# A seven-product MLP behind an attention: copies of two transposed tiles, and the order of the last products, moved

## The chip, the cores and the metric

The kernel runs on one core of one Trainium2 chip. The metric is the device time of one execution in microseconds (us), as the median of three runs. The core has five engines that run side by side and wait for one another by semaphores: TensorE (PE; its weight loads are PEld), VectorE (DVE), ScalarE (ACT), GpSimd (POOL) and SyncE (SP), the last of which only issues DMAs here. Each engine works off its own queue in order: an instruction that waits holds up everything queued behind it on that engine.

## The reference

An attention whose scores are masked by a hash of q and k, followed by a block that mixes with a Fourier transform, normalises, and applies a two-layer MLP. What matters here is the second part, with x of shape (4 batches, 768 rows, 512 columns):

```python
X = np.fft.fft(np.fft.fft(x, axis=1), axis=2)
u = x + np.real(X)
un = (u - mean(u)) / np.sqrt(var(u) + 1e-06)
ch = np.maximum(un @ w_ch1, 0.0) @ w_ch2      # 512 -> 2048 -> 512
return u + ch
```

## The kernel before, in words

**Stages.** First comes the attention for all four batches (to about 338 us). Then each batch b = 0 to 3 goes through `mlp7` (line 1442), which applies the two layers of the MLP; `front` (line 1055), the Fourier part of the next batch, runs beside it. Products of large blocks are done by a scheme that needs seven products of quarter blocks where the plain one needs eight. The quarters of the left and right factor are added and subtracted first, and the seven results are added and subtracted into the four quarters of the result.

**First layer.** Its result is the tile `hall`, with the quarters c11, c12, c21 and c22. It is made in two halves of the 2048 hidden features. Batches 0 and 1 use seven products per block row (lines 1538 to 1563). Batches 2 and 3 go through `two_levels` (line 1646), where each of the seven products (A11, S2, A12, S1, S3, A22, S4) is again split into seven leaves, j = 0 to 6. `ring_ahead` (line 1575) fixes the order of the 49 leaves of a half: product n and leaf j are sorted by 7n + 2j, so that the end of one product overlaps the beginning of the next. A leaf is four matmul instructions in the profile (line 1739). Its left factor comes by DMA into a ring of 12 slots. A product has three PSUM tiles, each a bank: `run`, used by leaves 0, 2, 4 and 6, one for leaf 1, and one for leaves 3 and 5. Leaf 2 adds into `run` in place, so it may start only when leaf 0's result has been read out; the same holds for leaves 4 and 6.

`placed` (line 1685) takes a leaf's result out of PSUM. The first six products of the order go into a quarter or a spare tile (table `to`, line 1666), in part by copies on ACT (line 1669), in part by adds on DVE (line 1675). The last product, S4, is added straight into its final place c12 by seven adds on DVE, with a ReLU on ACT (line 1672) behind four of them. `behind` (line 1712) holds the adds of whole quarters that follow the seventh leaf of a product.

**Second layer.** `outer7` (line 1365) is called for each half and works on three pairs of row tiles, j = 0 to 2: tile j, whose sum row is u, and tile j + 3, whose sum row is v. A pair is seven products of eight matmuls (line 1392). `tile_sums` (line 1366) makes the left sums on DVE: s1 from c12 and c22 (line 1376), s2 from s1 and c11 (line 1377), s3 from c11 and c12 (line 1378). The names a11, a12, a21, a22 stand there for parts of c11, c21, c12 and c22. So c21 goes only into the product `a12` and into the sum of line 1416. Results are added into u and v, scaled by the row's 1/deviation (line 1404), and in the second half stored to the output (`store`, line 939; on POOL's queue for batches 0 to 2, on SP's for batch 3).

**The tiles u and v.** `across` (line 1187) transposes a row tile of x on PE into a PSUM tile, and ACT copies it out (line 1193) into a buffer `ut[T]`. These buffers are shared between batches: the copy for batch b must wait until the store of batch b - 1 has read the same buffer. In batches 2 and 3, tiles 0, 3, 1 and 4 are copied in `first_parts`; tiles 2 and 5 at the beginning of `two_levels` (lines 1650 and 1651), ahead of the first leaf. `last_parts` (line 1171) then makes the last sums of the right factor on DVE.

**What sets the order.** The attention's order is as written. For all that comes after it, a planner puts each engine's instructions in order when the program is built; it prefers what stands earlier in the program, and takes something later when the earlier one is not ready by its own estimate. Where the code says `with in_turn():` (line 694) the instructions inside are queued behind the last recorded copy or ReLU of ACT and the last recorded add of DVE. PSUM has eight banks, and after the attention all tiles in it come from one pool of eight (line 1217).

Of the kernel before, what the change touches and what calls it, by code (L numbers as in the profile page):

```python
# [17 lines left out]
ALU = mybir.AluOpType  # L18
AX = mybir.AxisListType

P = 128
# [11 lines left out]
GT = GTT * P  # L33
# [450 lines left out]
def _main(  # L484
# [13 lines left out]
    nc = tc.nc  # L498
# [191 lines left out]
    ET = mybir.EngineType  # L690
# [493 lines left out]
        parted(b, xv[:, 0:1, 1], 6)  # L1184
        third(xv[:, :, 1])

    def across(b, T, u):

        x = xs[b]
        ps = pt([P, NDC, P], f"un{b}_{T}")  # L1190
        for c in range(NDC):
            nc.tensor.transpose(ps[:, c, :], x[:, c, T * P : (T + 1) * P], ident)
        nc.scalar.copy(u, ps.rearrange("p c n -> p (c n)"))

    def spread(b, T, u):

        bs = wt([P, 6], F32, "bs", f"bs{b}_{T}")
        nc.vector.bn_stats(bs, u)  # L1198
        mv = wt([P, 2], F32, "mv", f"mv{b}_{T}")
        nc.vector.bn_aggr(mv, bs)  # L1200
        rs = wt([P, 1], F32, "rs", f"rs{b}_{T}", NT)
        nc.gpsimd.tensor_scalar(rs, mv[:, 1:2], 1e-6, None, op0=ALU.add)
        nc.gpsimd.tensor_tensor(rs, rs, mhalf, op=ALU.pow)
        return rs
# [124 lines left out]
    def blocks2():  # L1329

        for half in range(2):
# [18 lines left out]
            for i in range(7):  # L1350
# [11 lines left out]
                )  # L1362
                yield

    def outer7(b, half, hall, ut, rs, s1s):
        def tile_sums(j):
            if half == 0:
                for T in (j, j + GT):
                    if T not in rs:
                        rs[T] = spread(b, T, ut[T])  # L1370
            a11, a12, a21, a22 = (
                hall[:, i, :, (j + g * GT) * P : (j + g * GT + 1) * P]
                for g in range(2) for i in range(2)
            )
            s1, s2 = s1s[j % 2], s2s[j % 2]
            nc.vector.tensor_tensor(s1, a21, a22, op=ALU.add)  # L1376
            nc.vector.tensor_tensor(s2, s1, a11, op=ALU.subtract)
            nc.vector.tensor_tensor(a21, a11, a21, op=ALU.subtract)
            return a11, a12, a21, a22, s1, s2

        nxt = tile_sums(0)
        for j in range(GT):
            a11, a12, s3, a22, s1, s2 = nxt
            u, v = ut[j], ut[j + GT]
            ru, rv = rs[j], rs[j + GT]

            def product(a, i, ps=None):
                start = ps is None
                if start:
                    ps = pt([P, HD], f"o{b}_{half}_{j}_{i}")  # L1390
                for r in range(HF // 2):
                    nc.tensor.matmul(  # L1392
                        ps, a[:, r], right7[i][:, r], start=start and r == 0,
                        stop=r == HF // 2 - 1, skip_group_check=not start,
                    )
                if j == GT - 1 and (b < B - 1 if half else b > 0):
                    nc.sync.dma_start(right7[i], bd[1 - half, i])
                return ps

            low, high = slice(0, HD), slice(HD, DM)  # L1400
            t6, t7 = (temps[j % 2][:, i] for i in range(2))

            def add(t, r, cols, src):
                done_by[ET.DVE] = nc.vector.scalar_tensor_tensor(  # L1404
                    t[:, cols], src, r, t[:, cols], op0=ALU.mult, op1=ALU.add
                )


            px = product(a11, B11)
            add(u, ru, low, px)  # L1410
            yield
            p2 = product(a12, B21)
            add(u, ru, low, p2)
            if half:
                store(b, j, u, low)
            nc.vector.tensor_tensor(a12, a12, s2, op=ALU.subtract)
            product(s2, T2, px)
            done_by[ET.Activation] = nc.scalar.copy(t6, px)  # L1418
            yield
            add(u, ru, high, t6)  # L1420
            p5 = product(s1, T1)
            add(v, rv, high, p5)
            product(s3, T3, px)
            done_by[ET.Activation] = nc.scalar.copy(t7, px)  # L1424
            add(v, rv, high, t7)
            if half:
                store(b, j + GT, v, high)
            yield
            if j < GT - 1:
                nxt = tile_sums(j + 1)  # L1430
            product(a12, B22, p5)
            add(u, ru, high, p5)
            if half:
                store(b, j, u, high)
            yield
            product(a22, T4, px)
            add(v, rv, low, px)
            yield
            if half:
                store(b, j + GT, v, low)  # L1440
# [133 lines left out]

    def ring_ahead():

        order = [A11, S2, A12, S1, S3, A22, S4]
        leaves = sorted(
            (half, 7 * n + 2 * j, i, j)
            for half in range(2)  # L1580
            for n, i in enumerate(order)
            for j in range(7)
        )
        fetched = [0]

        def fetch():
            if fetched[0] < len(leaves):
                half, _, i, j = leaves[fetched[0]]
                j = LEAVES[j]
                if isinstance(j, str):  # L1590
                    a, k = int(j[1]) - 1, int(j[2]) - 1
                    f = half * HF // 2 + a
                    src = ad[f : f + 3 : 2, i, :, k].rearrange("g p m -> p g m")
                else:
                    src = ad2[half, i, j]
                nc.sync.dma_start(ring[fetched[0] % NR], src)
                fetched[0] += 1

        for _ in range(NR):
            fetch()  # L1600
        return leaves, fetch
# [44 lines left out]
    def two_levels(b, right, ut, ss):  # L1646

        leaves, fetch = rings.pop(b)
        ut += [u4[b], wt([P, DM], F32, "u", f"u{b}_5", 2)]
        for T in (2, 5):  # L1650
            across(b, T, ut[T])
        last_parts(b)
        parts = {}
        for i, r in right.items():
# [8 lines left out]
        (c11, c12), (c21, c22) = (  # L1663
            [hall[:, i, :, g * HALF : (g + 1) * HALF] for g in range(2)] for i in range(2)
        )
        to = {A11: c12, S2: q0, A12: q1, S1: c22, S3: q0, A22: q1, S4: c12}

        def copy(d, s_):
            done_by[ET.Activation] = nc.scalar.copy(d, s_)  # L1669
# [4 lines left out]
        def add(d, x, y):  # L1674
            done_by[ET.DVE] = nc.vector.tensor_tensor(d, x, y, op=ALU.add)  # L1675
# [9 lines left out]
        def placed(i, j, ps):  # L1685

            y = to[i]
            y00, y01, y10, y11 = (
                y[:, a::2, c * HH : (c + 1) * HH] for a in range(2) for c in range(2)
            )  # L1690
            run, p2, p5 = (ps.get(n) for n in range(3))
            if i == S4:
                d = (y00, y00, y01, y11, y11, y01, y10)[j]
                add(d, d, (run, p2, run, p5, run, p5, run)[j])
                if j in (1, 4, 5, 6):
                    relu(d)
            elif j == 0:
                copy(y00, run)
            elif j == 1:
                add(y00, y00, p2)  # L1700
            elif j == 2:
                copy(y01, run)
            elif j == 3:
                copy(y11, p5)
            elif j == 4:
                add(y11, y11, run)
            elif j == 5:
                add(y01, y01, p5)
            else:
                copy(y10, run)  # L1710

        def behind(i):

            if i == S2:
                added(c21, c12, q0)
            elif i == A12:
                added(c11, c12, q1, relu)
            elif i == S1:
                added(c12, c21, c22)
            elif i == S3:  # L1720
                added(c21, c21, q0)
                added(c22, c22, c21, relu)
            elif i == A22:
                added(c21, c21, q1, relu)

        rs = {}

        def inner(half):
            banks_ = {}
            for n, (h_, _, i, j) in enumerate(leaves):  # L1730
                if h_ != half:
                    continue
                ps = banks_.setdefault(i, {})
                at_bank = (0, 1, 0, 2, 0, 2, 0)[j]
                start = at_bank not in ps
                if start:
                    ps[at_bank] = pt([P, 2, HH], f"h{b}_{half}_{i}_{at_bank}")
                for g in range(2):
                    nc.tensor.matmul(  # L1739
                        ps[at_bank][:, g], ring[n % NR][:, g], parts[i][j],  # L1740
                        start=start and g == 0, stop=g == 1, skip_group_check=True,
                    )
                fetch()
                placed(i, j, ps)
                if j == 6:
                    behind(i)
                if n in (24, 32):
                    T = 0 if n == 24 else GT
                    with in_turn():
                        rs[T] = spread(b, T, ut[T])  # L1750
                if n % 49 % 4 == 3:
                    yield
# [120 lines left out]
```

## Time and profile before

| | |
|---|---|
| median of 3 runs (lowest, highest) | 1011.06 us (1009.11, 1013.58) |
| the profiled execution's own time | 1011.05 us |
| its span in the profile | 1009.3 us |
| attention until about | 338 us |
| first layer of batch 2: first half, second half begin at | 693.74 us, 769.81 us |
| first layer of batch 3: first half, second half begin at | 860.70 us, 933.49 us |
| share of the span: PE, DVE, ACT, POOL | 98%, 72%, 48%, 10% |
| mean granted TensorE clock | 0.997 |

How to read it: times are us from the span's start; lines such as L1739 are lines of the kernel before. In a timeline a row is a run of like instructions: start, time until the last one's modelled end, engine, line, operation, output<-inputs, shape, count, and in brackets how long the engine stood idle before it and what released it. Matmuls overlap in the pipeline, so their pace is read from one row's start to the next row's start, not from the second column. A wait list names who waited for whom, the total in us, how often, and the longest.

### The profile page before, as it was taken

How to read it: one execution, taken by the hardware profiler on the slowest of the kernel's cores; microseconds unless marked ns; L12 is line 12 of the kernel's file. 1: busy time of each engine (PE TensorE's matmuls, PEld its weight loads, DVE VectorE, ACT ScalarE, POOL GpSimd, SP SyncE). 2: the span in 40 equal slices, each digit the busy share in tenths (PEclk: the TensorE clock that was granted, in tenths of full speed). 3: DMA queues.
4: the chain of work that ended last, by engine and by line, in shares of the span. 5: the costliest groups of instructions: out<-in, count | busy, mean ns of one | idle time of the engine just before them, and what ended most of it. 6: DMA issues, size and time to landing. Idle time of an engine off the chain costs nothing.

```text
span 1009.3 us, 15350 instructions
## 1 busy us (share of the span) xinstructions
PE 986.1 (98%) x5505; PEld 692.2 (69%) x5505; DVE 724.4 (72%) x1272; ACT 483.1 (48%) x933; POOL 96.7 (10%) x193
## 2 busy tenths in 40 slices
PE   8999999999999999999999999998999999899997
PEld 5444444444444756866885785897989899888986
DVE  4788898878986597778653686455897846693672
ACT  5787877878766465055035323212633521330420
POOL 3000000000000011320212130011220002010000
PEclk9999999999999999999999999999999999999999
DMA  9545362554510448567645495106838603743701
GB/s 145 122 96 110 87 160 53 123 96 100 127 45 10 151 120 286 168 191 265 204 154 170 139 328 172 54 21 214 261 98 277 185 22 109 219 117 105 228 28 46
DMA packets 207141, 141.37 MB, mean 140 GB/s; under 512 B 128464, under 2 KB 190416, under 8 KB 207056
## 3 DMA queue, kind: packets, MB, share of 16 engines
q1 hardware_dynamic: 196464, 106.48, 38.4%
q0 software_dynamic: 9024, 33.43, 10.8%
q8 instruction: 46, 0.75, 0.3%
q10 hardware_dynamic: 1568, 0.39, 0.2%
q14 instruction: 39, 0.32, 0.1%
HBM read 111.94 MB, written 28.31 MB: 139 GB/s over the span
## 4 chain that ended last, share of the span: by engine, by line
PE 87%; DVE 4%; DMA 3%; issue 3%; ACT 1%; POOL 1%; SPq 0%; DVEq 0%; POOLq 0%; ACTq 0%
PE o L1392 25%; PE oo L875 13%; PE h L1739 13%; PE sc L858 12%; PE h_px L1500 6%; PE h_p L1500 5%; PE sc L848 4%; PE cs L1073 3%; PE A L1102 2%; PE B L1102 2%; DMA zraw<-in_moe_w_ch_dram 2%; PE sum L895 1%; PE bits L812 1%; DMA out_dram<-w 1%; DVE bs L1198 1%
## 5 line engine op out<-in xcount | busy, mean ns | idle before, releaser
L1392 PE MATMUL o<-w,h 128*128 128x256 f32 x960 | 217.5, 379 | 0.1
L1392 PEld LDWEIGHTS o<-w,h 128*128 128x128 f32 x960 | 180.7, 190 | 24.6 <-DVE u L1404 0.7
L865 ACT ACTIVATE pk<-sc 128x768 f32<-128x768 f32 x192 | 152.6, 813 | 34.8 <-PE sc L858 31.4
L858 PE MATMUL sc<-qt,kt 64*128 64x384 f32 x768 | 155.5, 482 | 0.0
L875 PE MATMUL oo<-pk,vn 128*64 128x385 f32 (+1 forms) x768 | 134.4, 492 | 0.0
L932 DVE TENSOR_TENSOR acc<-acc,pk 128x1536 f32<-128x1536 f32 x63 | 110.1, 1748 | 3.1
L875 PEld LDWEIGHTS oo<-pk,vn 128*64 128x64 f32 x768 | 50.9, 136 | 81.1 <-issue 79.2
L858 PEld LDWEIGHTS sc<-qt,kt 64*128 64x128 f32 x768 | 69.5, 188 | 30.5 <-issue 30.0
L1418 ACT COPY tq<-o 128x256 f32<-128x256 f32 x24 | 8.9, 373 | 149.8 <-PE o L1392 149.8
L1404 DVE SCALAR_TENSOR_TENSOR w<-o,rs,w 128x256 f32<-128x256 f32 x88 | 42.2, 480 | 49.3 <-PE o L1392 48.6
L1739 PE MATMUL h<-sums,w 128*128 128x192 f32 x336 | 61.0, 328 | 6.5 <-ACT h L1669 6.5
L1739 PEld LDWEIGHTS h<-sums,w 128*128 128x128 f32 x336 | 55.5, 190 | 8.0 <-ACT h L1669 7.5
L848 PEld LDWEIGHTS <-kk 33*128 33x128 bf16 x384 | 19.6, 93 | 50.8 <-issue 28.6
L1739 PE MATMUL h<-x,w 128*128 128x192 f32 x256 | 52.4, 330 | 0.9 <-DVE h L1675 0.9
L1392 PE MATMUL o<-w 128*128 128x256 f32 x176 | 42.7, 381 | 4.1 <-DVE w L1376 4.1
L1392 PE MATMUL o<-w,tq 128*128 128x256 f32 x192 | 45.5, 380 | 0.4 <-DVE w L1404 0.4
L1739 PEld LDWEIGHTS h<-x,w 128*128 128x128 f32 x256 | 43.4, 192 | 2.7 <-DVE h L1675 2.0
L1424 ACT COPY tq<-o 128x256 f32<-128x256 f32 x24 | 8.9, 373 | 72.8 <-PE o L1392 69.7
L1675 DVE TENSOR_TENSOR h<-h,h 128x384 f32<-128x384 f32 x52 | 28.6, 551 | 20.1 <-PE h L1739 13.3
L1392 PEld LDWEIGHTS o<-w,tq 128*128 128x128 f32 x192 | 36.3, 190 | 5.9 <-DVE w L1404 0.8
L1739 PE MATMUL h<-w 128*128 128x192 f32 x192 | 40.2, 333 | 0.0
L1392 PEld LDWEIGHTS o<-w 128*128 128x128 f32 x176 | 32.9, 190 | 9.7 <-issue 3.3
(210 smaller groups left out, 1635.6 us busy)
## 6 DMA issues: line engine op xcount, KB each, us to landing
w<-ad SPq DMA_DIRECT2D x252, 128.0 KB, 2.6
w<-bd SPq DMA_DIRECT2D x42, 512.0 KB, 4.9
zraw<-in_moe_w_ch_dram SPq DMA_DIRECT2D x16, 512.0 KB, 4.5
zraw<-in_moe_w_ch_dram POOLq DMA_DIRECT2D x16, 512.0 KB, 4.0
bd<-w SPq DMA_DIRECT2D x14, 512.0 KB, 5.7
vn<-in_v_dram SPq DMA_DIRECT2D x32, 192.0 KB, 3.1
qn<-in_q_dram SPq DMA_DIRECT2D x116, 48.0 KB, 3.2
kn<-in_k_dram SPq DMA_DIRECT2D x58, 96.0 KB, 3.0
```

Of the source, the lines that this page charges most:

```text
L848: nc.tensor.matmul(pss[g][:, h, 0:HALF], kk[r, ks], bits[1][r] if g else bits[0][r, h], start=start, stop=not start,)
L858: nc.tensor.matmul(pss[g][:, h, 0:HALF], kt[rows, ks], qt[rows, g * HALF : (g + 1) * HALF], start=early, stop=not early,)
L865: nc.scalar.activation(pk[:, g, :, 0:HALF], pss[g][:, :, 0:HALF], AF.Exp, scale=SCALE)
L875: nc.tensor.matmul(oos[g][h * D : (h + 1) * D, 0:w], nat["v", n][:, (2 * c + h) * D : (2 * c + h + 1) * D], pk[:, g, h, 0:w], start=(c == ...
L932: nc.vector.tensor_tensor(acc, (first[:, :, :, 0:HALF] if c == 1 else acc), new, op=ALU.add)
L1073: nc.tensor.matmul(ps[:, pc + 2 * lo : pc + 2 * hi - 1 : 2], z[:, cp, pc, par, t * P : (t + 1) * P], ch[:, cp, pc, lo:hi], start=(cp == 0) ...
L1102: nc.tensor.matmul(ps[:, cols], F[:, par, k, t, j * P : (j + 1) * P], sq[:, t, k, cols], start=(t == 0), stop=(t == 1),)
L1392: nc.tensor.matmul(ps, a[:, r], right7[i][:, r], start=start and r == 0, stop=r == HF // 2 - 1, skip_group_check=not start,)
L1404: done_by[ET.DVE] = nc.vector.scalar_tensor_tensor(t[:, cols], src, r, t[:, cols], op0=ALU.mult, op1=ALU.add)
L1500: nc.tensor.matmul(ps, left[:, k], right[i][:, k], start=start and k == 0, stop=k == 1, skip_group_check=not start,)
L1675: done_by[ET.DVE] = nc.vector.tensor_tensor(d, x, y, op=ALU.add)
L1739: nc.tensor.matmul(ps[at_bank][:, g], ring[n % NR][:, g], parts[i][j], start=start and g == 0, stop=g == 1, skip_group_check=True,)
```

## The change

Three things are changed. In `two_levels` the transposes of tiles 2 and 5 stay where they are, but their copies from PSUM are handed back as functions and called inside the first half of the first layer, behind the leaves at places 10 and 14 of the order, under `in_turn`. The order of the seven products becomes A11, S2, A12, S1, S3, S4, A22: A22 is now the last and is added straight into c21, while S4 goes through the spare tile `q1` into c12. In `outer7` the order of the seven products of a pair becomes a11, s1, s2, a12, s3, (a12 - s2), a22, where it was a11, a12, s2, s1, s3, (a12 - s2), a22; the difference a12 - s2 is written over s2 instead of over a12; and `tile_sums` becomes a function of its own, called for the first pair of batches 2 and 3 already in the first layer, behind leaf 5 of A22. The count of instructions on each engine stays as it is.

```diff
-    def across(b, T, u):
+    def across(b, T, u, later=False):
         x = xs[b]
         ps = pt([P, NDC, P], f"un{b}_{T}")
         for c in range(NDC):
             nc.tensor.transpose(ps[:, c, :], x[:, c, T * P : (T + 1) * P], ident)
-        nc.scalar.copy(u, ps.rearrange("p c n -> p (c n)"))
+        def end():
+            nc.scalar.copy(u, ps.rearrange("p c n -> p (c n)"))
+        if later:
+            return end
+        end()
...
+    def tile_sums(b, half, hall, ut, rs, s1s, j):
+        if half == 0:
+            for T in (j, j + GT):
+                if T not in rs:
+                    rs[T] = spread(b, T, ut[T])
+        a11, a12, a21, a22 = (
+            hall[:, i, :, (j + g * GT) * P : (j + g * GT + 1) * P]
+            for g in range(2) for i in range(2)
+        )
+        s1, s2 = s1s[j % 2], s2s[j % 2]
+        nc.vector.tensor_tensor(s1, a21, a22, op=ALU.add)
+        nc.vector.tensor_tensor(s2, s1, a11, op=ALU.subtract)
+        nc.vector.tensor_tensor(a21, a11, a21, op=ALU.subtract)
+        return a11, a12, a21, a22, s1, s2
+
+    early = {}
+
     def outer7(b, half, hall, ut, rs, s1s):
...
-        nxt = tile_sums(0)
+        nxt = early.pop((b, half), None) or tile_sums(b, half, hall, ut, rs, s1s, 0)
...
             px = product(a11, B11)
             add(u, ru, low, px)
             yield
+            p5 = product(s1, T1)
+            add(v, rv, high, p5)
+            product(s2, T2, px)
+            done_by[ET.Activation] = nc.scalar.copy(t6, px)
+            add(u, ru, high, t6)
+            nc.vector.tensor_tensor(s2, a12, s2, op=ALU.subtract)
+            yield
             p2 = product(a12, B21)
             add(u, ru, low, p2)
             if half:
                 store(b, j, u, low)
-            nc.vector.tensor_tensor(a12, a12, s2, op=ALU.subtract)
-            product(s2, T2, px)
-            done_by[ET.Activation] = nc.scalar.copy(t6, px)
-            yield
-            add(u, ru, high, t6)
-            p5 = product(s1, T1)
-            add(v, rv, high, p5)
             product(s3, T3, px)
...
-                nxt = tile_sums(j + 1)
-            product(a12, B22, p5)
+                nxt = tile_sums(b, half, hall, ut, rs, s1s, j + 1)
+            product(s2, B22, p5)
...
-        order = [A11, S2, A12, S1, S3, A22, S4]
+        order = [A11, S2, A12, S1, S3, S4, A22]
...
-        for T in (2, 5):
-            across(b, T, ut[T])
+        ends = [across(b, T, ut[T], True) for T in (2, 5)]
...
-        to = {A11: c12, S2: q0, A12: q1, S1: c22, S3: q0, A22: q1, S4: c12}
+        to = {A11: c12, S2: q0, A12: q1, S1: c22, S3: q0, S4: q1, A22: c21}
...
-            if i == S4:
+            if i == A22:
...
-            elif i == A22:
-                added(c21, c21, q1, relu)
+            elif i == S4:
+                added(c12, c12, q1, relu)
...
+                if n in (10, 14):
+                    with in_turn():
+                        ends.pop(0)()
+                if i == A22 and j == 5:
+                    early[b, half] = tile_sums(b, half, hall, ut, rs, ss, 0)
```

More of the change, by code (lines that the diff above doesn't have):

```diff
@@ L1363, in blocks2 @@
                 yield
-    def outer7(b, half, hall, ut, rs, s1s):
[L1366 to L1379, printed above, removed]
-        nxt = tile_sums(0)
+    def tile_sums(b, half, hall, ut, rs, s1s, j):
[13 more added lines that the diff above has]
+    early = {}
+    def outer7(b, half, hall, ut, rs, s1s):
+        nxt = early.pop((b, half), None) or tile_sums(b, half, hall, ut, rs, s1s, 0)
         for j in range(GT):
```

## The prediction

> **What bounds the kernel now.** I read the page's first part, then the list of PE's waits, then the timeline around each of them.
>
> ```profile
> span 1009.3 us, 15350 instructions
> PE 986.1 (98%) x5505; PEld 692.2 (69%) x5505; DVE 724.4 (72%) x1272; ACT 483.1 (48%) x933; POOL 96.7 (10%) x193
> PE h L1739 <- ACT h L1669: 6.5, 2, 3.8
> PE o L1392 <- DVE w L1376: 4.1, 4, 1.3
> PE h L1739 <- DVE h L1675: 0.9, 2, 0.5
> 564.99 36.26 PE o L1392 x168
> ```
>
> PE sets the time. The last row, from the chain of work, is one half of the second layer of batch 1: 168 matmuls in 36.26 us, 0.216 us each with no gap. No instruction of PE is removed, so all that can be won is PE's idle and slow time, and the three wait rows name nearly all of it in the code that the diff touches: 6.5 us at the first layer behind a copy of ACT, 4.1 us at the second layer behind s1 (L1376), 0.9 us at leaves behind DVE. Now the first of them, in batch 2:
>
> ```profile
> 692.12 0.54 POOL L947 DMA_DIRECT2D out_dram<-w  x1 [0.71 <-DVE w L1404]
> 693.84 0.54 POOL L947 DMA_DIRECT2D out_dram<-u  x1 [1.18 <-DVE u L1404]
> 697.99 0.59 ACT L1193 COPY w<-un 128x512 f32<-128x512 f32 x1 [7.95 <-DMA out_dram<-w]
> 698.47 0.48 ACT L1669 COPY h<-h 128x384 f32<-128x384 f32 x1
> 698.99 0.59 ACT L1193 COPY u<-un 128x512 f32<-128x512 f32 x1
> 693.74 1.47 PE L1739 MATMUL h<-x,w 128*128 128x192 f32 x8
> 699.01 1.74 PE L1739 MATMUL h<-sums,w 128*128 128x192 f32 x8 [3.81 <-ACT h L1669]
> 704.04 0.81 PE L1739 MATMUL h<-x,w 128*128 128x192 f32 x4
> 699.65:703.05 3.40, 3.40 (x14) 3.40 (x13) 0.00 (x0) 1.44 (x3) 0.00 (x0) 0.59 0.28 77
> ```
>
> The copy of tile 2 waits 7.95 us for batch 1's store out of the same buffer, issued at 692.12. Behind it in ACT's queue stands the copy of leaf 0, which leaf 2 needs, so PE does leaves 0 and 1 (8 matmuls) and stands for 3.81 us. The last row (PE, PEld, DVE, ACT, POOL busy; granted clock, DMA share, GB/s) adds the second half of the damage: after the idle time the granted clock is 0.59. Batch 3 has the same stall, shorter, and the second half of each batch starts without these copies (the first row here is the ring's loads, median us to landing last):
>
> ```profile
> w<-ad SPq DMA_DIRECT2D x252, 128.0 KB, 2.6
> 860.70 1.47 PE L1739 MATMUL h<-x,w 128*128 128x192 f32 x8
> 864.88 1.57 PE L1739 MATMUL h<-sums,w 128*128 128x192 f32 x8 [2.71 <-ACT h L1669]
> 868.23 0.81 PE L1739 MATMUL h<-x,w 128*128 128x192 f32 x4
> 863.86 0.59 ACT L1193 COPY w<-un 128x512 f32<-128x512 f32 x1 [7.18 <-DMA out_dram<-w]
> 933.49 1.46 PE L1739 MATMUL h<-x,w 128*128 128x192 f32 x8
> 938.23 0.81 PE L1739 MATMUL h<-x,w 128*128 128x192 f32 x4
> ```
>
> **Part 1: the two copies move behind leaves 10 and 14.** Between the first and the last PE row of each start lie the same 28 matmuls. They take 938.23 - 933.49 = 4.74 us in an undisturbed half, 704.04 - 693.74 = 10.30 us in batch 2 and 868.23 - 860.70 = 7.53 us in batch 3. The stalls cost 5.56 and 2.79 us, together **8.35 us**. Do the copies wait again where they go? A leaf is four of the 28 matmuls, 0.68 us, so leaf 10 ends 11 x 0.68 = 7.4 us after the start. That is 701.1 in batch 2, with the store landed by 697.99: 3 us of margin; and 868.1 against 863.86, 4 us, in batch 3. The other store (tile 5's, issued 693.84) was in by 698.99 and its copy comes four leaves later, at 703.9. Ring loads (128 KB each) will now start while the stores are under way; I let that eat 1 to 2 us of the margin. What is then late next is only leaf 2 behind leaf 0's copy, as in the second halves, which is in the 4.74 us. The copies hold two of eight PSUM banks for 11 to 15 leaves. By then A11 and S2 have opened six more at most, and A11's second bank is free after one add, so I cost it at nothing; bound: a bank freed one add of DVE (0.55 us) late at each start, 1.1 us. In ACT's stream they are 2 x 0.59 us beside gaps; the copy queued behind each is needed four leaves (2.6 us) later: nothing.
>
> How much of this a timed execution holds is less sure for the clock: the stall's 5.56 us are 3.81 idle and 1.75 slow. By the Trainium skill, "TensorE: Matmul & The Clock Gate", Part 1, the clock halves after an idle window of about 3.4 us, and the windows run freely; so by it a stall of 3.81 us would close the gate in some executions only. The trace has it closed after 3.81 us and open after 2.71 us, and agrees so far; what the rule would give is rival 5.
>
> **Part 2: A22 last, s1 early.** Today's end of the first layer, batch 3, second half (behind one row of the page on the adds into u and v):
>
> ```profile
> L1404 DVE SCALAR_TENSOR_TENSOR w<-o,rs,w 128x256 f32<-128x256 f32 x88 | 42.2, 480 | 49.3 <-PE o L1392 48.6
> 963.62 0.59 PE L1392 MATMUL o<-w,h 128*128 128x256 f32 x2
> 964.70 1.89 PE L1392 MATMUL o<-w,h 128*128 128x256 f32 x8
> 967.10 0.59 PE L1392 MATMUL o<-w,h 128*128 128x256 f32 x2
> 967.54 0.81 PE L1739 MATMUL h<-sums,w 128*128 128x192 f32 x4
> 968.19 1.03 PE L1392 MATMUL o<-w,h 128*128 128x256 f32 x4
> 970.48 1.53 PE L1392 MATMUL o<-w 128*128 128x256 f32 x6 [1.27 <-DVE w L1376]
> 966.61 0.54 DVE L1675 TENSOR_TENSOR h<-h,h 128x384 f32<-128x384 f32 x1
> 968.39 0.56 DVE L1675 TENSOR_TENSOR h<-h,h 128x384 f32<-128x384 f32 x1 [0.53 <-PE h L1739]
> 968.98 0.52 ACT L1672 ACTIVATE h<-h 128x384 f32<-128x384 f32 x1 [0.56 <-DVE h L1675]
> 969.65 1.28 DVE L1376 TENSOR_TENSOR w<-h 128x512 f32<-128x512 f32 x2
> 895.10 1.03 PE L1392 MATMUL o<-w,h 128*128 128x256 f32 x4
> 896.55 0.92 PE L1739 MATMUL h<-x,w 128*128 128x192 f32 x4 [0.42 <-DVE h L1675]
> 898.38 1.46 PE L1392 MATMUL o<-w,h 128*128 128x256 f32 x6
> 900.61 1.53 PE L1392 MATMUL o<-w 128*128 128x256 f32 x6 [0.77 <-DVE w L1376]
> ```
>
> s1 hangs on the last leaf: leaf (967.54 to 968.19), add 968.39, ReLU 968.98, s1 969.65, PE 970.48. By starts, four matmuls from 968.19 end at 969.05: 1.43 us lost. In the first half (last four rows) 0.93 us is lost at 900.61 and 0.59 at 896.55. Batch 2 has the same waits (the wait list counts four and two). So about 2 x 1.43 + 2 x 1.52 = 5.9 us stand here.
>
> With A22 last, s1 needs c12 and c22, done one product earlier: it can follow the fifth leaf's add, at about 968 instead of 969.65. But the cover shrinks too. Today PE fills the gaps between the last leaves with both products a11 and a12: 12 matmuls before the last leaf, 4 behind. a12 needs c21, which is now the late quarter, so only the 8 of a11 are left: 4 x 0.216 = 0.86 us of new idle before the last leaf, whose own time is set by DVE's add at 966.61 as today. Behind it, s1's product starts at once or up to 0.3 us late. I get about 0.9 to 1.1 us lost in place of 1.43 to 1.52, and less if DVE takes that add ahead of the first result of the second layer (L1404, 0.48 us). I take a gain of **0.55 us** at each of the four places, **2.2 us**. Bounds: all 5.9 us go; or s1 comes no earlier, and a product less of cover (1.73 us) makes each place worse by that: -6.9 us.
>
> **Part 3: the new order in all pairs.** Between pairs nothing shows: the planner makes a later pair's sums far ahead (the two L1376 at 969.65 are for two pairs), each reuse of a PSUM bank keeps a whole product between read and write, and a12 - s2 has two products of cover, 3.5 us, for an operation of s1's shape (0.69 us below). What is left are the four half starts of batches 0 and 1, where s1 is wanted after one product, not two. Worst is batch 0's second half:
>
> ```profile
> 471.25 3.62 PE L1392 MATMUL o<-w,h 128*128 128x256 f32 x16
> 471.84 0.93 ACT L1523 ACTIVATE h<-h 128x384 f32<-128x384 f32 x2
> 472.93 0.69 DVE L1376 TENSOR_TENSOR w<-h 128x512 f32<-128x512 f32 x1
> ```
>
> s1 is done at 473.62; a11 ends at 471.25 + 1.73 = 472.98: 0.6 to 0.8 us of idle, unless the planner puts a12 in between. The other three have s1 in time. I take **-0.4 us** (bounds 0 and -0.8 with a little for the first half of batch 0). Stores are the same in number; one of four comes two products later, under PE's work.
>
> **Sum:** 8.35 + 2.2 - 0.4 = 10.15 us, from the profiled execution's 1011.05 (span 1009.3 and 1.75 around it; the median is 1011.06): **1001 us**.
>
> **The rivals.**
> 1. All waits vanish, the ends of the first layer too: 8.35 + 5.9 = 14.2 us, 996.8. For it: s1's product and c21 no longer hang on one chain. Against it: only 8 matmuls cover the last leaves.
> 2. The start is won, the end is lost: s1 stays as late relative to the last leaf, or DVE, busy through that stretch, makes s1, s2, s3 ahead of leaf 6's add and delays it. About -1 us at each of four places: 8.35 - 4 - 0.4 = 4 us, 1007; half of that, 1005.
> 3. The change doesn't do what it says: the copies still block ACT, because with leaves running the ring loads (one every 0.68 us) push the stores' landing 3 us and more out, past 701. Then a landing later by d costs d - 3 - 2.6 us; or the planner moves them. Gain 0 to 4 us: about 1009. Against it: DMA has room (share 0.28 in the windows row, after the stall).
> 4. Slower: at all eight half starts one product of cover (1.73 us) is lost because s1 is not made early; 8 x 1.73 = 13.8 us against 8.35: 1016.5. It outweighs the start's gain from 1.04 us per half start on. Against it: three of the four in batches 0 and 1 have s1 in time.
> 5. The half clock is missing in the timed executions of the kernel before: then 1.75 us less is won, 8.4 us, 1002.7. For it: batch 3 stalls without it. Against it: the profiled execution, which has it, took the median's time.
>
> **How the numbers follow.** Forecast (999 to 1002.5) 0.42; rival 5 0.10; rival 1 0.13; rival 2 0.17, mostly under 1006; rival 3 0.14; rival 4 0.04. The range 996.5 to 1006.2 takes in all but rivals 3, 4 and the worst of 2. Faster by over 0.5% (below 1006.0, about what a measurement here can tell from no change): 0.42 + 0.10 + 0.13 + 0.14 (of rival 2) = 0.79. Within: 0.03 + 0.14 = 0.17. Slower: 0.04.
>
> **What would show it.** Right: no wait of PE on ACT at L1739 over 0.3 us; clock 1.00 just after batch 2 starts; 28 matmuls in about 4.8 us in all four halves; the two copies of tiles 2 and 5 with no DMA as releaser. For part 2, a wait of about 0.9 us before the last leaf and little before s1's product. Wrong: a DMA releaser at those copies, a PE wait on a bank at leaves 11 to 15, or waits on L1376 that grew.

## The result and the profile after

The changed kernel takes **1002.56 us** in the median of four executions (1001.95 to 1002.72), the kernel before in the same comparison 1011.06 in the median of three (1009.11 to 1013.58). A fourth execution of the kernel before took 1721.01 us and is left out of these figures. The ratio is **0.9913**, 95% interval 0.9885 to 0.9941: faster by 0.9%, some 8.8 us. The profiled execution took 1002.41 us, its span is 8.8 us shorter than before's. The page's first part, and the two rows of PE's wait list that concern the edited code (lines have moved: leaves are L1746, products of the second layer L1400, s1 L1381, leaf adds L1682, `across` L1195):

```profile
span 1000.5 us, 15339 instructions
PE 985.1 (98%) x5505; PEld 692.2 (69%) x5505; DVE 724.2 (72%) x1272; ACT 481.7 (48%) x933; POOL 96.6 (10%) x193
```
```profile
PE o L1400 <- DVE w L1381: 1.8, 5, 0.5
PE h L1746 <- DVE h L1682: 1.3, 4, 0.4
```

The row of 6.5 us behind ACT is gone. The row of s1 has fallen from 4.1 to 1.8, the row of leaves behind DVE has risen from 0.9 to 1.3. Now PE's timeline of the changed kernel, where the four half starts of batches 2 and 3 are, and, in the two first halves, the leaf that is the 29th to 32nd matmul:

```profile
695.04 1.47 PE L1746 MATMUL h<-x,w 128*128 128x192 f32 x8
...
699.78 0.81 PE L1746 MATMUL h<-x,w 128*128 128x192 f32 x4
...
764.47 1.46 PE L1746 MATMUL h<-x,w 128*128 128x192 f32 x8
...
854.93 1.47 PE L1746 MATMUL h<-x,w 128*128 128x192 f32 x8
...
859.67 0.81 PE L1746 MATMUL h<-x,w 128*128 128x192 f32 x4
...
924.86 1.46 PE L1746 MATMUL h<-x,w 128*128 128x192 f32 x8
```

The 28 matmuls of a start take 699.78 - 695.04 = 4.74 us in batch 2 and 859.67 - 854.93 = 4.74 in batch 3, where they took 10.30 and 7.53. With the starts of before (shown above), each half can be compared:

| from start to next start, us | before | after | difference |
|---|---|---|---|
| batch 2, first half | 76.07 | 69.43 | -6.64 |
| batch 2, second half | 90.89 | 90.46 | -0.43 |
| batch 3, first half | 72.79 | 69.93 | -2.86 |
| batch 3, second half, to the end of the span | 75.81 | 75.64 | -0.17 |
| all that lies ahead of batch 2 | 693.74 | 695.04 | +1.30 |

So 10.1 us are won from batch 2 on, 8.35 of them at the two starts, and 1.3 lost ahead of it. The stores and the copies that caused the stall, from the timelines of POOL and ACT of the changed kernel:

```profile
693.42 0.54 POOL L947 DMA_DIRECT2D out_dram<-w  x1 [0.72 <-DVE w L1412]
695.15 0.54 POOL L947 DMA_DIRECT2D out_dram<-u  x1 [1.19 <-DVE u L1412]
...
703.01 0.59 ACT L1195 COPY w<-un 128x512 f32<-128x512 f32 x1
...
704.70 0.60 ACT L1195 COPY u<-un 128x512 f32<-128x512 f32 x1
```

Neither copy has a releaser any more: it comes 9.6 us behind the issue of its store, and needed 5.9 before (issued 692.12, copy at 697.99). At the end of the first layer in batch 2's first half, PE and DVE of the changed kernel show what part 2 left:

```profile
726.88 1.47 PE L1746 MATMUL h<-w 128*128 128x192 f32 x8
728.63 0.92 PE L1746 MATMUL h<-sums,w 128*128 128x192 f32 x4 [0.29 <-DVE h L1682]
729.86 1.97 PE L1400 MATMUL o<-w 128*128 128x256 f32 x8 [0.31 <-DVE w L1381]
731.67 0.59 PE L1400 MATMUL o<-w,h 128*128 128x256 f32 x2
...
728.03 1.01 DVE L1682 TENSOR_TENSOR h<-h,h 128x384 f32<-128x384 f32 x2
729.03 0.69 DVE L1381 TENSOR_TENSOR w<-h 128x512 f32<-128x512 f32 x1
729.64 0.55 DVE L1682 TENSOR_TENSOR h<-h,h 128x384 f32<-128x384 f32 x1
```

s1 (729.03) now goes ahead of the last leaf's add (729.64), as hoped. But DVE works without a gap through this stretch, and PE waits for it twice. By starts the 12 leaf and 8 product matmuls take 731.67 - 726.88 = 4.79 us; without a stop they take 12 x 0.1625 + 8 x 0.216 = 3.68. The place still costs 1.11 us, though the brackets name only 0.29 + 0.31 of it.

### The profile page after: what moved, and what is told of

Read it like the earlier page. It is cut to its first block, busy times and chain, and to the rows that moved or that the text cites. A ratio compares the mean times of both kernels' runs of the same rounds, so it can differ in the third digit from the quotient of the medians.

```text
span 1000.5 us, 15339 instructions
## 1 busy us (share of the span) xinstructions
PE 985.1 (98%) x5505; PEld 692.2 (69%) x5505; DVE 724.2 (72%) x1272; ACT 481.7 (48%) x933; POOL 96.6 (10%) x193
## 4 chain that ended last, share of the span: by engine, by line
PE 89%; DVE 4%; DMA 2%; ACT 1%; issue 1%; POOL 1%; SPq 0%; DVEq 0%; POOLq 0%
PE o L1400 28%; PE oo L875 13%; PE sc L858 12%; PE h L1746 11%; PE h_px L1508 6%; PE h_p L1508 5%; PE sc L848 4%; PE cs L1073 3%; PE A L1102 2%; PE B L1102 2%; DMA zraw<-in_moe_w_ch_dram 2%; PE sum L895 1%; DVE h L1682 1%; PE bits L812 1%; PE un L1192 1%
## 5 line engine op out<-in xcount | busy, mean ns | idle before, releaser
L1400 PE MATMUL o<-w,h 128*128 128x256 f32 x768 | 176.6, 380 | 0.0
L1400 PEld LDWEIGHTS o<-w,h 128*128 128x128 f32 x768 | 145.3, 191 | 19.1
L1400 PE MATMUL o<-w,tq 128*128 128x256 f32 x384 | 91.0, 380 | 0.4 <-DVE w L1412 0.4
L1400 PEld LDWEIGHTS o<-w,tq 128*128 128x128 f32 x384 | 72.9, 190 | 10.6 <-DVE w L1412 1.1
L1746 PE MATMUL h<-sums,w 128*128 128x192 f32 x336 | 61.6, 330 | 0.9 <-DVE h L1682 0.9
L1746 PEld LDWEIGHTS h<-sums,w 128*128 128x128 f32 x336 | 55.1, 190 | 3.4 <-DVE h L1682 2.4
L1746 PE MATMUL h<-x,w 128*128 128x192 f32 x256 | 49.5, 326 | 0.0
L1400 PE MATMUL o<-w 128*128 128x256 f32 x176 | 42.0, 382 | 1.8 <-DVE w L1381 1.8
L1746 PEld LDWEIGHTS h<-x,w 128*128 128x128 f32 x256 | 42.9, 190 | 0.1
L1746 PE MATMUL h<-w 128*128 128x192 f32 x192 | 39.4, 329 | 0.4 <-DVE h L1682 0.4
L1400 PEld LDWEIGHTS o<-w 128*128 128x128 f32 x176 | 32.9, 190 | 7.3 <-PE h L1746 2.3
L1508 PE MATMUL h_px<-x,w 128*128 128x384 f32 x96 | 35.7, 490 | 0.3 <-ACT h L1555 0.3
```

What stands on the lines that cost most here:

```text
L1400: nc.tensor.matmul(ps, a[:, r], right7[i][:, r], start=start and r == 0, stop=r == HF // 2 - 1, skip_group_check=not start,)
L1508: nc.tensor.matmul(ps, left[:, k], right[i][:, k], start=start and k == 0, stop=k == 1, skip_group_check=not start,)
L1746: nc.tensor.matmul(ps[at_bank][:, g], ring[n % NR][:, g], parts[i][j], start=start and g == 0, stop=g == 1, skip_group_check=True,)
```

## The experiments

The theory after the result: the start of the first layer is worth 8.35 us and needs the copies' move alone; the new order wins some 1.8 us from batch 2 on, most of it at the ends of the first layer, and gives 0.7 back in batch 0. Rivals: the margin to the stores' landing decides; the early call decides; the half clock was an accident of one execution. In the first comparison the kernel before took 1010.45 us (1009.22 to 1011.97), in the second 1010.35 (1009.28 to 1013.31); each ratio is to the kernel before in its own comparison.

### The copies alone

```diff
-        order = [A11, S2, A12, S1, S3, S4, A22]
+        order = [A11, S2, A12, S1, S3, A22, S4]
```
with the second layer's order and `tile_sums` of the kernel before; the two late copies stay.

> The kernel before, with only the two copies moved behind leaves 10 and 14; both product orders as before. Theory (the parts are independent, and the copies are worth what they cost at the two starts): the 28 matmuls at the start of batches 2 and 3 take about 4.75 us each, no copy of tiles 2 and 5 waits for a store, the clock stays full, and 8.4 us are won: about 1002.7 us. The four waits for s1 stay at 0.8 to 1.3 us (4.1 in all). Rival (part of the start's gain needs the new order, for instance because the banks come free otherwise): less than 6 us won, above 1005 us.

Measured: 1002.62 us (1001.34 to 1003.99), ratio 0.9925 (0.9909 to 0.9942). PE's wait list of this kernel:

```profile
PE o L1398 <- DVE w L1382: 4.1, 4, 1.3
...
PE h L1744 <- DVE h L1680: 0.9, 2, 0.5
```

The wait on ACT is gone; the other two rows are those of the kernel before, to the tenth. Part 1 alone gives the whole result, within what a time can tell. Moving the copies is enough.

### The order alone

```diff
-        ends = [across(b, T, ut[T], True) for T in (2, 5)]
+        for T in (2, 5):
+            across(b, T, ut[T])
...
-                if n in (10, 14):
-                    with in_turn():
-                        ends.pop(0)()
```

> The changed kernel, with the two copies back ahead of the first leaf: only the orders are changed. Theory: the starts of batches 2 and 3 stall again by about 5.6 and 2.8 us, the ends of the first layer are 1.8 us shorter in sum and batch 0's second half 0.7 us longer: about 1 us won against before, 1010 us. Rival (the order does most of the work, the copies little): 1004 us or less. On the clock: if the gate goes by free-running windows, the half clock after a stall of about 3.8 us in batch 2 may be missing here (then 1.7 us less at that start); if every stall of that length closes it, it is there again.

Measured: 1011.76 us (1009.67 to 1012.29, ten executions), ratio 1.0008 (0.9998 to 1.0018): nothing won, a miss of about 1.8 us. The waits at the ends of the first layer fell as in the changed kernel (the rows read 1.8 and 1.3 again), so parts 2 and 3 did their work. The loss is at the starts. Windows of its profile (busy time of PE, PEld, DVE, ACT and POOL, granted clock, DMA share, GB/s):

```profile
694.44:697.85 3.41, 0.99 (x7) 0.69 (x5) 2.12 (x5) 0.36 (x1) 0.17 (x1) 1.00 0.99 376
697.85:701.26 3.41, 2.75 (x9) 2.75 (x10) 0.56 (x1) 1.67 (x4) 0.00 (x0) 0.50 0.22 69
701.26:704.68 3.42, 3.42 (x12) 3.42 (x11) 0.55 (x1) 0.96 (x2) 0.00 (x0) 0.50 0.34 109
861.69:865.10 3.41, 0.72 (x4) 0.72 (x5) 0.74 (x2) 1.02 (x3) 0.00 (x0) 1.00 0.81 308
865.10:868.51 3.41, 3.41 (x13) 3.41 (x12) 0.82 (x3) 1.87 (x4) 0.00 (x0) 0.50 0.29 77
```

The clock is half for 6.83 us behind the stall of batch 2 and for 3.41 behind that of batch 3: about 5.1 us of work lost, where the first profile of the kernel before loses 1.7 in this way. Is that the order's doing, or chance? The next runs ask.

### Three more profiles

The kernel with the order alone twice more, and the kernel before twice more, unchanged.

> The kernel before, profiled once more, for rival 5: is the half clock after batch 2's stall there in every execution? Theory (an idle time of 3.8 us closes the gate each time): a granted clock of about 0.6 in the 3.4 us behind the stall of batch 2 and 1.0 behind that of batch 3, span 1009 +-1. Rival (the windows run free, so that it hits some executions only): clock 1.0 behind both, and a span shorter by about 1.7.

> The new order with the copies in their old place, profiled once more, because its time missed. In its first profile the clock is half from 697.85 to 704.68 (6.83 us) and from 865.1 to 868.5 (3.4 us), and 49 lengths of 3.413 us lie between the two closings. Theory (the gate looks at windows of 3.41 us that run freely, so the place of a stall in them differs between executions, and a window closes it from about 2 us of idle PE on): the two starts again stand 3.1 to 3.3 us each, but the half clock begins elsewhere relative to the stall, and it lasts 0, 3.41 or 6.83 us; the span is 1005.5 to 1010.5. Rival (the new order itself brings the half clock, by what it leaves in the stall): 6.8 us and 3.4 us again, span 1010.

> The same kernel a third time. Theory: a third placing of the windows, half clock for whole multiples of 3.41 us, at least one of the two starts unlike the first profile in these two repeats. Rival: as the first profile.

> The kernel before a third time. In the two profiles so far the gate closed in the stall of batch 2 (3.81 and 3.14 us of idle time) at 700.27 and 699.27, and stayed open in that of batch 3 (2.71 and 2.80). Theory (free windows of 3.41 us, closing from about 2 us of idle PE in one window): half clock for 0 or 3.41 us behind either stall, by the place of the window; a stall of 2.7 to 2.8 us closes the gate in some executions too. Rival (the length of the stall decides, between 2.80 and 3.06 us): closed behind batch 2's stall, open behind batch 3's, as in both before.

One execution each: 1011.01 us, 1009.38, 1010.94 and 1009.41. PE's idle time at the two starts, and the half clock behind it:

| profile | batch 2: idle us, half clock us | batch 3: idle us, half clock us | span us |
|---|---|---|---|
| before, first | 3.81, 3.42 | 2.71, 0 | 1009.3 |
| before, second | 3.14, 3.41 | 2.80, 0 | 1009.2 |
| before, third | 3.52, 0 | 2.29, 0 | 1007.6 |
| order alone, first | 3.08, 6.83 | 3.06, 3.41 | 1010.2 |
| order alone, second | 2.91, 0 | 2.92, 3.41 | 1007.6 |
| order alone, third | 2.89, 3.41 | 2.78, 3.41 | 1009.2 |

The length of the stall doesn't decide: 2.78 us closed the gate once, 3.52 us did not. The third profile of before, PE's timeline, then three windows, the stall in the first two of them:

```profile
694.39 1.47 PE L1739 MATMUL h<-x,w 128*128 128x192 f32 x8
699.38 1.57 PE L1739 MATMUL h<-sums,w 128*128 128x192 f32 x8 [3.52 <-ACT h L1669]
```
```profile
694.19:697.60 3.41, 1.67 (x12) 1.37 (x10) 2.80 (x7) 0.00 (x0) 0.54 (x1) 1.00 0.94 327
697.60:701.02 3.42, 1.64 (x10) 1.64 (x11) 0.55 (x1) 2.06 (x5) 0.00 (x0) 1.00 0.40 140
701.02:704.43 3.41, 3.41 (x23) 3.41 (x22) 1.66 (x3) 1.06 (x3) 0.00 (x0) 1.00 0.53 166
```

In the theory the place of the stall in a row of windows decides. The two closings of the first profile of the order alone lie 865.10 - 697.85 = 167.25 us apart, 49 x 3.413. Laid out from a closing, in the five profiles that have one, the windows in which PE was busy for 0.27 to 1.26 of 3.41 us end with the clock halved, those with 1.47 and more without. The third profile of before fits as well: behind its last matmul the clock falls to 0.50 at 1004.80 us, and 91 windows of 3.413 us ahead of that lies 694.19. So the two windows shown above are in the row: the border cuts the stall of 3.52 us in two, PE is busy for 1.67 and 1.64 us, and the clock stays full. The two nearest to the border are both of the first profile of before, the first ahead of its closing, the second in batch 3's stall (700.27 to 860.70 is 47 windows):

```profile
696.86:700.27 3.41, 1.26 (x8) 1.26 (x9) 0.56 (x1) 1.86 (x4) 0.00 (x0) 1.00 0.40 143
700.27:703.69 3.42, 3.42 (x12) 3.42 (x12) 0.28 (x1) 1.13 (x3) 0.00 (x0) 0.50 0.41 115
860.70:864.11 3.41, 1.47 (x10) 1.17 (x8) 1.79 (x6) 0.25 (x1) 0.32 (x1) 1.00 0.98 376
```

So batch 3's stall of 2.71 us was spared: the border of a window cut it in two. The same is seen in the second profile of the order alone, where a stall of 2.91 us lies across a border and both windows stay at full clock behind it, with PE busy for 1.90 and 2.01 us:

```profile
694.44:697.86 3.42, 1.90 (x14) 1.61 (x12) 3.03 (x7) 0.00 (x0) 0.54 (x1) 1.00 1.00 377
697.86:701.27 3.41, 2.01 (x12) 2.02 (x13) 0.56 (x1) 2.33 (x5) 0.00 (x0) 1.00 0.45 152
```

The size of the miss agrees: each half window costs 1.7 us, and the three profiles of the order alone hold six of them, those of before two. Three profiles of each are few, but every timed execution has a mean granted clock on record. In the profiles of the table 0.999 goes with no half window, 0.997 with one and 0.994 with three. The ten executions of the order alone have 0.9952 in the mean, the thirteen of before 0.9972 (either holds some half clock behind the last matmul); over 1009 us that is 4.0 us more at half clock, 2.0 us of work. So the new order does make closings likelier. That it does so by evening out the stalls of batches 2 and 3 is only argued, and why batch 3's stall is some 0.3 us longer isn't shown.

### The copies behind leaves 2 and 4

```diff
-                if n in (10, 14):
+                if n in (2, 4):
```

> The changed kernel with the two copies behind leaves 2 and 4 instead of 10 and 14. It measures the margin of part 1. Theory (only the landing of batch 1's store counts, and all that stands behind the copy in ACT's queue waits with it): in the profile after, the two stores of batch 1's last tiles land at about 698.4 and 700.15 us, and leaves 2 and 4 end at about 697.1 and 698.5. So the copies wait 1 to 2 us in batch 2, about as long in batch 3, with a DMA as releaser, and PE stands 1 to 3 us in all, too short for the half clock: 1004 to 1005 us. Rival 1 (the place is of no weight once the copies are behind the first leaf, since leaf 0's copy then goes ahead of them): no wait of PE, 1002.6. Rival 2 (any wait of ACT here costs the whole stall): 1009 to 1011.

Measured: 1001.84 us (1001.63 to 1002.39), ratio 0.9916 (0.9895 to 0.9937): as the changed kernel, so rival 1. ACT's timeline in batch 2, the store's issue from POOL's, and PE's first 28 matmuls in the windows view:

```profile
692.16 0.54 POOL L947 DMA_DIRECT2D out_dram<-w  x1 [0.71 <-DVE w L1412]
...
696.12 0.48 ACT L1676 COPY h<-h 128x384 f32<-128x384 f32 x1 [1.01 <-PE h L1746]
697.39 0.58 ACT L1195 COPY w<-un 128x512 f32<-128x512 f32 x1 [0.79 <-DMA out_dram<-w]
697.87 0.49 ACT L1676 COPY h<-h 128x384 f32<-128x384 f32 x1
```
```profile
693.78:698.52 4.74, 4.74 (x30) 4.50 (x29) 3.20 (x8) 2.09 (x5) 0.54 (x1) 1.00 0.99 365
```

The copy does wait for the store, for 0.79 us, and PE loses nothing at this start; in batch 3 the other copy waits 0.66 us, and nothing is lost either. The store took 697.39 - 692.16 = 5.23 us to come free, with the ring loads running. The copies of leaves 0 and 2 are already past (leaf 1 is an add on DVE). The next one in the queue, leaf 3's, ends at 697.87 + 0.49 = 698.36, and the leaf that needs it, leaf 5 of A11, begins at 698.52, when the 28 matmuls are through: by these times a store 0.2 us later would have held PE. PE's wait list has one row that the changed kernel's lacks, 0.7 us behind a copy of ACT, but it lies at 772 us, in batch 2's second half, where no copy was moved. What decides is what stands behind a waiting copy and when it is due, not that the copy waits.

### Without the early call

```diff
-                if i == A22 and j == 5:
-                    early[b, half] = tile_sums(b, half, hall, ut, rs, ss, 0)
```

> The changed kernel without the early call of the left sums behind leaf 5 of the last product: they are made where the second layer begins, as for the other pairs. It asks whether the early call or the new last product brings s1 forward. Theory (s1 no longer hangs on the last leaf, and the planner puts it where it is ready, wherever the program names it): the same as the changed kernel, 1002.6, PE's wait on s1 at the four ends 0.4 to 0.65 us. Rival (the early call does it): s1 comes after the last leaf again, waits of about 1.4 us, 1005 to 1006.

Measured: 1002.73 us (1002.19 to 1004.91), ratio 0.9921 (0.99 to 0.9943): the same. PE's wait list:

```profile
PE un L1192 <- DVE x L1116: 2.0, 2, 1.5
PE o L1400 <- DVE w L1381: 1.8, 5, 0.5
...
PE h L1746 <- DVE h L1682: 1.3, 4, 0.4
...
PE h L1746 <- DMA w<-ad: 0.5, 1, 0.5
```

The two rows of the ends are unchanged. The profiled execution is longer by 2.6 us (span 1003.1), and the first and the last row, neither of them at the edited place, are 2.5 of it. So the early call isn't what brings s1 forward; by what is left, the new last product does.

### One more product as cover

In batches 2 and 3, the product a11 of the second pair is issued right behind that of the first, and the second pair uses it in place of one of its own.

```diff
+            if j == 0 and b >= TWO:
+                ahead[1] = product(
+                    hall[:, 0, :, P : 2 * P], B11, name=f"o{b}_{half}_1_ahead"
+                )
```

> The changed kernel, with one more product to fill PE at the end of the first layer of batches 2 and 3: the first product of the second pair (its left factor is part of c11, finished long before) is issued right behind that of the first pair. Theory (at these four places PE lacks 8 matmuls of cover that it had before; the last leaf waits for DVE, and there is nothing else to do): the idle time there falls from 3.65 us in sum (0.93, 0.85, 1.22, 0.85 less what was noise) to under 1.2 us, and the time to about 999.8 us. Rival (DVE limits the whole stretch, so that what PE does in the gap is missing as cover behind it): the idle time only moves to s1's, s2's or a later product, and the time stays within 0.6 us of 1002.4.

Measured: 997.22 us (996.73 to 997.93), ratio 0.9868 (0.9852 to 0.9884), some 5 us better than the changed kernel and 2.6 better than expected. PE's timeline at the end of batch 2's first half:

```profile
726.75 1.46 PE L1753 MATMUL h<-w 128*128 128x192 f32 x8
728.05 1.03 PE L1401 MATMUL o_ahead<-w,h 128*128 128x256 f32 x4
728.91 0.81 PE L1753 MATMUL h<-sums,w 128*128 128x192 f32 x4
729.56 1.03 PE L1401 MATMUL o_ahead<-w,h 128*128 128x256 f32 x4
730.43 0.81 PE L1401 MATMUL o<-w 128*128 128x256 f32 x3
```

The same 12 leaf and 8 product matmuls now take 730.43 - 726.75 = 3.68 us, the undisturbed time, against 4.79. The second product fills both gaps. The brackets of the changed kernel name 2.55 us at the four ends, and the expectation counted 3.65, of which it left 1.2 standing. By starts it is 1.11 us here and 5.0 in the four (the spans differ by 5.1), and all of it is gone.

### The old order in batches 0 and 1

```diff
-            p5 = product(s1, T1)
-            add(v, rv, high, p5)
+            if b < TWO:
+                p2 = product(a12, B21)
+                add(u, ru, low, p2)
...
+            else:
+                p5 = product(s1, T1)
+                add(v, rv, high, p5)
```
and the reverse two products later.

> The changed kernel, with a12 ahead of s2 and s1 in the second layer of batches 0 and 1 (as before, but for the sum a12 - s2, which stays in s2), and the new order in batches 2 and 3. Theory (batch 0's second half loses 0.7 us because s1 is wanted after one product): the wait before s1's product in that half is gone, its second layer takes 36.1 us again, not 36.84, and the time is 0.7 us lower, about 1001.7. Rival (the 0.7 us is a chance of that execution): it is there again, or comes and goes without the order.

Measured: 1001.41 us (1000.73 to 1002.88), ratio 0.9913 (0.9897 to 0.993): too little to be told by the time. PE's timeline at batch 0's second half tells it; first the changed kernel, then this one:

```profile
471.74 1.89 PE L1400 MATMUL o<-w,h 128*128 128x256 f32 x8
474.16 2.00 PE L1400 MATMUL o<-w 128*128 128x256 f32 x8 [0.53 <-DVE w L1381]
```
```profile
470.70 3.62 PE L1400 MATMUL o<-w,h 128*128 128x256 f32 x16
474.15 1.96 PE L1400 MATMUL o<-w,tq 128*128 128x256 f32 x8
```

In the changed kernel eight matmuls (1.73 us) take 474.16 - 471.74 = 2.42: 0.69 lost. With the old order sixteen take 3.45, and nothing is lost.

### Both together

The cover in batches 2 and 3 and the old order in batches 0 and 1.

> The two gains put together: the a11 product of the second pair as cover at the ends of the first layer in batches 2 and 3, and the old order of the seven products in batches 0 and 1. If they are independent it is the time with the cover (997.2) less the 0.7 us that the old order wins in batch 0's second half: 996.5. Rival (the old order of batches 0 and 1 lets batch 1's stores land later and the starts of batch 2 stall again): 998 or more, with a wait of PE in batch 2's start.

Measured: **996.07 us** (995.78 to 996.45), ratio 0.9857 (0.9836 to 0.9878), the fastest version here: 14.3 us under the kernel before of its comparison. Of the waits on s1 and on leaf adds none is left; its wait list begins in the first layer of batches 0 and 1:

```profile
PE h_px L1525 <- ACT h L1572: 1.2, 2, 1.0
```

The span is 994.5 us, against 995.4 with the cover alone.

## Why the prediction was right, point by point

The prediction was 1001.0 us, the time 1002.56; the mechanism held, and the sum was 10.15 us against 8.8 in the spans and 8.5 in the medians. The time lies in the range, but just above the forecast's own band (999 to 1002.5): parts 2 and 3 fell short by 0.45 and 0.4 us, and 0.5 us were in no step.

**Part 1, 8.35 us: right.** The two starts won 5.56 and 2.79. The copies don't wait where they went, as reckoned, with 3 to 4 us of margin to the stores' landing. The run with leaves 2 and 4 shows that the margin wasn't needed in full: there one copy waits 0.79 us, and nothing is lost. The cause of the stall is the copy of leaf 0 that stood behind the waiting copy, as the part on the bound said. Rival 3 is refuted: neither copy waits for its store in the changed kernel, and with the ring loads running a store came free in 5.23 us, against 5.87 before (692.12 to 697.99). The banks cost nothing: no wait at leaves 11 to 15.

**The size of part 1 depends on the execution: rival 5 in few.** Rival 5's time, 1002.7 us, came out nearly, but not for its reason. Its half clock was missing in two of the thirteen timed executions of before (granted clock 0.999); the others have 0.996 or 0.997. The third profile of before has the stall without the half clock, and a span of 1007.6, 1.7 us less than the first. By the Trainium skill, "TensorE: Matmul & The Clock Gate", Part 1, the gate's window is 3413 ns and runs freely; the closings 49 x 3.413 us apart and half clocks of 3.41 and 6.83 us agree. The same part of the Trainium skill asks for at least one idle window of about 3.4 us before the clock is halved; here a window with PE busy for 1.26 of its 3.41 us was idle enough, so the measurement decides. The profile that the sum was made against was one with the half clock.

**Part 2, 2.2 us: right in kind, about 1.75 in size.** From the table, less 8.35, 1.75 us are left for the four ends and the tail. The prediction had 0.9 to 1.1 us left standing at each end; the cover run, which frees them, won 5.0 us in all, 1.1 to 1.6 at each. What failed is "s1's product starts at once or up to 0.3 us late". In the rows of batch 2's first half above, 0.45 us are lost before the last leaf (0.86 were reckoned), 0.58 before s1's product and 0.08 in it: DVE's back-to-back adds hold both the last leaf and s1, and each stop costs more than its bracket. The gain is uneven: 1.08 (6.64 - 5.56) in batch 2's first half and only 0.07 (2.86 - 2.79) in batch 3's. Some 0.3 of the 1.08 didn't lie at the end of the first layer at all. In the kernel before, the last 24 matmuls of batch 2's first half take 769.81 - 764.30 = 5.51 us where 24 x 0.216 are 5.18:

```profile
764.30 5.68 PE L1392 MATMUL o<-w,h 128*128 128x256 f32 x24
```

The changed kernel's last 40 there, from 755.84 to 764.47, take 8.63, their undisturbed time. So some 1.4 us are left for the four ends; what held PE at those 24 isn't shown. Rival 1 is what the cover brought: all waits there gone.

**Part 3, -0.4 us: the mis-sized term.** The working found 0.6 to 0.8 us for batch 0's second half and took 0.4, for the chance that the planner would put a12 in between. It didn't: 0.69, and about 0.1 in batch 1. Between pairs the changed kernel loses nothing, as said. Rival 4 (1.73 us at each half start) is refuted.

**What no step held:** the first eight products of the second layer in batch 0 start 0.48 us later than before. These are the rows of the changed kernel and of the kernel before, from PE's timelines:

```profile
396.79 1.46 PE L1400 MATMUL o<-w,h 128*128 128x256 f32 x6
```
```profile
396.31 1.89 PE L1392 MATMUL o<-w,h 128*128 128x256 f32 x8
```

Nothing the diff orders runs ahead of this place, and in the other two profiles of the kernel before the same work comes 0.9 us later than in the first, in the copies alone 0.8 us earlier. So the 0.48 us lie within what differs between executions of one kernel. With 10.1 won from batch 2 on, less 0.8 for part 3 and 0.5 here, the 8.8 us are accounted for.

## What to carry to other kernels

An instruction that may wait for a transfer belongs behind the work of its engine's queue that others need soon: it may even wait there, for as long as the next one behind it isn't due. Before a new order takes independent work away from beside a wait, count the work that is left to cover it; one product issued ahead was worth more here (5.0 us) than the reordering that took its cover away (1.8). And read what a stop costs from start to start, not from the bracketed idle time, which named 0.60 of 1.11 us.

## What was not expected of the hardware

The clock gate is no matter of a stall's length alone. Over windows of 3.41 us, those with PE busy for 1.26 us or less were followed by a halved clock, those with 1.47 or more were not, so a stall of 2.78 us was punished and one of 3.52 us was not. One window with 2.75 us of work at half clock did not open the gate again, which cost a second one. So these two kernels, with stalls of 2.3 to 3.8 us, have times that differ between executions of the same program by about 1.7 us for each halved window, and two profiles are better than one.
